# A recurrent attention and a mixture of depths in one kernel: first decays loaded by two queues, two vectors loaded as rows, fewer products of zeros

## The chip, the cores and the metric

The kernel runs on one core of a Trainium2 chip. The metric is the device time of one execution in microseconds (us), as the median of several runs.

## What is computed

The reference chains two blocks. The first is a recurrence with a decay for each channel, over 4 batches, 8 heads, 768 steps and a head width of 48. For each step, with a state of 48x48 for each batch and head:

```python
cur = np.einsum('bhd,bhe->bhde', u[None] * kt, vt)
y[:, :, t] = np.einsum('bhd,bhde->bhe', rt, state + cur)
state = wt[:, :, :, None] * state + np.einsum('bhd,bhe->bhde', kt, vt)
```

Its outputs, the 8 heads side by side, are the rows x (4 batches of 768 rows of 384) of the second block. There each row gets a score `x @ w_gate`. In each batch the 128 rows with the highest scores go through two matrices, `relu(xe @ w1) @ w2` with 1024 in the middle; the result times the sigmoid of the score is added to the row. All other rows are put out as they are. Everything is fp32.

## The kernel before

**Tiling.** The 768 steps of a batch are cut into 6 chunks of 128, so there are 24 chunks, numbered n. For each chunk the kernel loads r, k, v and w as tiles of 128 steps by 8 heads by 48 channels, in buffers with 64 places for each head (`r_bufs`, `k_bufs`, `w_bufs`: 4 each; `v_bufs`: 5). The 16 spare places are filled once (1 for w, 0 for the others) with `nc.any.memset`, which picks an engine (line 130).

**One chunk.** TensorE transposes w (`decays_t`, into `ps_w`), so that the steps lie along the free axis. VectorE runs two scans over the decays (`scans`): `right` at line 255 and `left` at line 266, with two small operations between them. k and r are transposed too (`inputs_t`, into `ps_t`) and multiplied by the scans' results (`scaled`, line 313), which gives `K` and `R`; for the first two chunks `K` is made by a copy on ScalarE (`src`) and a multiplication on GpSimd instead (`scaled_aside`). `scores` multiplies K and R into `ps_s` (line 349), `masked` applies the causal mask on VectorE (`sc`, line 357), and `outputs_t` multiplies by v and by the state into `ps_yt` (lines 382 and 390), which ScalarE copies to `yt`. `ps_s` and `ps_yt` share one buffer of PSUM. `back` transposes K again (copied to `kt` by ScalarE), and `carry_products` and `carry` make the next state. `range_check` runs over w on ScalarE (`junk`, line 302).

**The bonus of u.** The term with u touches a step's own value alone: `own_products` (line 325, r times k) and `own_weights` (line 328, times `u_bc`) on GpSimd, `own_values` (8 sums on ScalarE, line 334), `own_results` on GpSimd. `u_bc` holds u in all 128 partitions; one DMA puts it there, which reads the same 384 values 128 times (`_rows(u, L)`).

**Rows out and scores.** `rows_out` transposes `yt` back, adds the bonus, and stores x. `row_products` multiplies x by `wg_bc` (GpSimd, line 419), the gate's vector in all partitions, which is loaded in the same way. `row_sums` adds up on ScalarE, and `compared` ranks the scores (`ahead`, line 491). `mixture` and `forward` gather the chosen rows and run the two matrices; their products are fed piecewise between those of later chunks.

**Order.** The order is written out by hand. `turn(i)` calls the steps of chunks i-1 to i+2 in the order in which each engine gets them, for i from -2 to 24. All loads and stores are issued by SyncE (SP) in one row, in program order: first the decays of chunk 0 as two halves of the heads, then the list in lines 150 to 161, with `u_bc` after k of chunk 1 and `wg_bc` after w of chunk 3; later loads are issued by `loads(i + 5)` at the end of a turn.

**Products of zeros.** `warm(n)` lets TensorE multiply a tile of zeros (`nothing`, bf16, 128x512) n times into a PSUM tile that nobody reads. It is called with 6 ahead of the first turn, and within the turns -2, -1 and 0:

```python
        if i == 0:
            warm(6)
```

Of the kernel before, what the change touches and what calls it, by code (L numbers as in the profile page):

```python
# [10 lines left out]
FP32 = mybir.dt.float32  # L11
# [7 lines left out]
L = 128  # L19
# [6 lines left out]
def _rows(ap, n):  # L26

    return dataclasses.replace(ap, ap=[[0, n]] + [list(x) for x in ap.ap])
# [10 lines left out]
def kernel(  # L39
# [40 lines left out]
    nc = tc.nc  # L80
    PSUM = bass.MemoryType.PSUM

    B, H, S, D = r.shape
    C = H * D
# [12 lines left out]
    consts = ctx.enter_context(tc.tile_pool(name="consts", bufs=1))  # L97
    setup = ctx.enter_context(tc.tile_pool(name="setup", bufs=1))
# [7 lines left out]
    psM = ctx.enter_context(tc.tile_pool(name="psM", bufs=1, space=PSUM))  # L106
# [14 lines left out]
    r_bufs = [consts.tile([L, H, DP], FP32, name=f"r_buf{i}") for i in range(NBUF)]  # L121
    k_bufs = [consts.tile([L, H, DP], FP32, name=f"k_buf{i}") for i in range(NBUF)]
    w_bufs = [consts.tile([L, H, DP], FP32, name=f"w_buf{i}") for i in range(NBUF)]
    v_bufs = [consts.tile([L, H, DP], FP32, name=f"v_buf{i}") for i in range(VBUF)]
    nothing = setup.tile([L, 512], BF16)
    nc.vector.memset(nothing, 0.0)
    for i in range(VBUF):
# [4 lines left out]
    def load(bufs, x, n):  # L132
        if n < N:
            b, ci = chunks[n]
            nc.sync.dma_start(  # L135
                out=bufs[n % len(bufs)][:, :, 0:D],
                in_=x[b, :, ci * L:(ci + 1) * L, :].rearrange("h t d -> t h d"),
            )

    def loads(n):  # L140
        load(v_bufs, v, n - 2)
        load(k_bufs, k, n - 1)
        load(r_bufs, r, n - 1)
        load(w_bufs, w, n)


    for hs in (slice(H // 2, H), slice(0, H // 2)):
        nc.sync.dma_start(
            out=w_bufs[0][:, hs, 0:D], in_=w[0, hs, 0:L, :].rearrange("h t d -> t h d")
        )  # L150
    for bufs, x, n in (
        (k_bufs, k, 0), (r_bufs, r, 0), (w_bufs, w, 1), (k_bufs, k, 1),
    ):
        load(bufs, x, n)
    u_bc = consts.tile([L, H, D], FP32)
    nc.sync.dma_start(out=u_bc, in_=_rows(u, L))
    for bufs, x, n in ((r_bufs, r, 1), (w_bufs, w, 2), (v_bufs, v, 0)):
        load(bufs, x, n)
    loads(3)
    wg_bc = consts.tile([L, C], FP32)  # L160
    nc.sync.dma_start(out=wg_bc, in_=_rows(moe_w_gate, L))
    w1 = consts.tile([L, NDC, F], FP32)
    w2 = consts.tile([L, NFC, C], FP32)

# [8 lines left out]
    def load_weights(n):  # L173
        while n > 0 and weights:
            to, src = weights.pop(0)
            nc.sync.dma_start(out=to, in_=src)
            n -= 1
# [3 lines left out]
    make_identity(nc, ident)  # L181
    minus = consts.tile([L, 1], BF16)
    nc.vector.memset(minus, -1.0)
    ones_f = consts.tile([L, 1], FP32)
    nc.vector.memset(ones_f, 1.0)
    high = consts.tile([L, 1], FP32)
# [2 lines left out]
    row = setup.tile([L, L], INT32)  # L189
# [6 lines left out]
    for t, sign in ((before_f, 1), (after_f, -1)):  # L196
        nc.gpsimd.memset(t, 1.0)
        nc.gpsimd.affine_select(
            out=t, in_=t, pattern=[[sign, L]], base=-1, channel_multiplier=-sign,
# [32 lines left out]
    def warm(n):  # L232

        ps = psM.tile([L, 512], FP32, tag="m", name="ps_n")
        for _ in range(n):
            nc.tensor.matmul(ps, nothing[:, 0:L], nothing, start=True, stop=True)


    def transposed(pool, tag, src):
# [36 lines left out]
    def check_sums():  # L276

        above = setup.tile([L, 1], FP32)
        nc.vector.tensor_reduce(out=above, in_=guard, axis=AX.X, op=ALU.add)
        below = setup.tile([L, 1], FP32)  # L280
        junk = setup.tile([L, N * HP], FP32)
        nc.vector.tensor_scalar(
            out=junk, in0=alls.rearrange("p n j -> p (n j)"), scalar1=float(LOW ** L),
            scalar2=None, op0=ALU.is_lt, op1=ALU.add, accum_out=below,
        )
        return above, below
# [342 lines left out]
    def step(f, n, *more):  # L629
        if 0 <= n < N:  # L630
            f(work.setdefault(n, dict(n=n)), *more)

    def mix(n=1, place=None):


        while n > 0 and mixing:
            if place is not None and mixing[0][1] not in (None, place):
                return
            try:
                mixing[0][1] = next(mixing[0][0])  # L640
                n -= 1
            except StopIteration:
                mixing.pop(0)
# [16 lines left out]
    def fed_in_turn(n, few):  # L660

        kept = (feed or picked) and (feed or picked)[0][0] == B - 2
        fed(few if kept else n, on=False)
# [6 lines left out]
    def turn(i):  # L670
        soon = i >= N - 1
        step(first_left, i + 1)
        if i < 1:
            step(scaled_aside, i + 1, "K", "right")
        step(own_products, i + 1)
        step(scores, i)
        step(own_values, i)
        step(carry, i - 1, work.get(i))
        if i > 0:
            step(scaled, i + 1, "K", "right")  # L680
        step(own_weights, i + 1)
        if soon:
            step(masked, i)
        if i == N - 1:
            sums.extend(check_sums())
        if i < N:
            step(compared, i - 2)
        if not soon:
            step(masked, i)
        step(back, i)  # L690
        if i == 0:
            warm(6)
        mix(place="half")
        step(rows_out, i - 1, soon)
        step(row_scores_soon if soon else row_products, i - 1)
        step(own_results, i)
        fed_in_turn(PIECES // 2, 2 if i >= N - 1 else 1)
        step(inputs_t, i + 1, "R", r_bufs)
        if i == -1:
            warm(2)  # L700
        step(scaled, i + 1, "R", "left")
        step(decays_t, i + 2)
        mix(place="mid")
        if i == -2:
            warm(2)
        step(range_check, i + 2)
        step(outputs_t, i)
        step(carry_products, i)
        fed_in_turn(PIECES - PIECES // 2, 1 if i == N - 1 else 0)
        if i == N - 1:  # L710
            step(compared, i - 1)
        step(inputs_t, i + 2, "K", k_bufs)
        if i == -2:
            warm(1)
        if not soon:
            step(row_sums, i - 1)
        step(scans, i + 2)
        if 0 <= i - 2 < N - 1 and chunks[i - 2][1] == NCH - 1:
            mixing.append([mixture(chunks[i - 2][0]), "end"])
        mix(place="end")  # L720
        if i > -2:
            loads(i + 5)
        if i in WEIGHT_TURNS:
            load_weights(1)

    with tc.manual_schedule():
        warm(6)
        for i in range(-2, N + 1):
            turn(i)

        ended.append(True)
        mix(1000)
        mixing.append([mixture(B - 1), "half"])
        step(compared, N - 1)
        fed(1)
        mix()
        wide = checked(sums)
        fed(1)
        mix()
        fed(NFC - 2)  # L740
        mix(2)
        fed(2)
        mix(1000)
        fed(1000)
        outside = nc.values_load(wide, min_val=0, max_val=1)
# [72 lines left out]
```

## Time and profile before

| | |
|---|---|
| time, median of 3 runs | 205.34 us (205.33 to 205.54) |
| the profiled execution's own time | 205.87 us |
| its span in the profile | 204.2 us |
| busy in the span: TensorE (PE) | 191.8 us (94%) |
| VectorE (DVE) | 160.8 us (79%) |
| GpSimd (POOL) | 135.7 us (66%) |
| ScalarE (ACT) | 124.6 us (61%) |
| loads and stores on SP's queue | 27.14 MB, 73.6% of 16 DMA engines' span |
| chain that ended last, by engine | PE 77%, SP's queue 7%, DMA 6%, DVE 4% |

In the profile's lines the first number is the start and the second the duration, both in us from the span's start; then come the engine, the line of the kernel, the operation and the tiles, written tile first. "xN" is the number of instructions merged into a line. In square brackets stands how long the engine was idle ahead of the line, and what ended that. "SPq" is SyncE issuing a DMA. In a table of windows each engine has its busy time and, in brackets, its number of instructions in that stretch; the last three columns are the granted clock, the DMA share and GB/s.

### The profile page before, as it was taken

Reading aid. Unit: us, or ns where it says so; the run is one execution under the profiler, and the core shown is the slowest. Engines: PE = TensorE matmul, PEld = TensorE weight load, DVE = VectorE, ACT = ScalarE, POOL = GpSimd, SP = SyncE. Lnnn points to the kernel's source line nnn. Section 1 sums busy time; section 2 is a strip of 40 time slices with the busy share of each in tenths; the row PEclk is TensorE's granted clock in tenths of the full one; section 3 lists DMA queues with packets and bytes.
Section 4 is the critical chain, followed back from the end, with each engine's and each line's share of the span. In section 5 each row is a group of like instructions: output and inputs, shape, how many; then the busy total and the mean of one; then the engine's idle time right before and its main releaser. Section 6 shows DMA issues by size and latency. Waiting matters only on the chain.

```text
span 204.2 us, 6418 instructions
## 1 busy us (share of the span) xinstructions
PE 191.8 (94%) x2292; PEld 156.2 (76%) x2293; DVE 160.8 (79%) x352; ACT 124.6 (61%) x644; POOL 135.7 (66%) x167
## 2 busy tenths in 40 slices
PE   7999999999899899999999999999999999999980
PEld 3577888877687688888877888898887888876940
DVE  5989899999999968988969788988879784961010
ACT  7287877768954776868454866878355866510300
POOL 6586898886867995777538898678528898111301
PEclk9999999999999999999999999999999999999997
DMA  6999999798989999999992994978672221111101
GB/s 111 186 163 173 176 187 204 173 223 151 257 161 251 171 216 218 174 206 240 200 199 57 189 171 108 154 146 158 126 121 65 55 79 42 39 42 42 39 8 43
DMA packets 105671, 29.20 MB, mean 143 GB/s; under 512 B 100512, under 2 KB 104864, under 8 KB 105632
## 3 DMA queue, kind: packets, MB, share of 16 engines
q1 hardware_dynamic: 105120, 27.14, 73.6%
q0 software_dynamic: 512, 1.57, 2.6%
q8 instruction: 20, 0.33, 0.8%
q14 instruction: 19, 0.16, 0.3%
HBM read 23.20 MB, written 5.51 MB: 141 GB/s over the span
## 4 chain that ended last, share of the span: by engine, by line
PE 77%; SPq 7%; DMA 6%; DVE 4%; ACT 2%; issue 2%; POOL 0%; POOLq 0%; DVEq 0%; ACTq 0%
PE ps_t L242 12%; PE ps_h L595 11%; PE ps_f L607 11%; PE ps_s L349 11%; PE ps_yt L382 10%; DMA k_buf<-in_k_dram 6%; SPq L135 5%; PE ps_yt L390 5%; PE ps_y L242 5%; PE ps_w L242 4%; PE ps_kv L444 4%; PE ps_e L485 3%; PE ps_r L511 1%; PE ps_x L559 1%; DVE left L266 1%
## 5 line engine op out<-in xcount | busy, mean ns | idle before, releaser
L334 ACT ACTIVATE rk<-rk 128x48 f32<-128x48 f32 x192 | 43.7, 231 | 0.0
L414 POOL TENSOR_TENSOR x<-x,vo 128x384 f32<-128x384 f32 x22 | 22.1, 1007 | 21.6 <-ACT x L412 21.3
L334 ACT ACTIVATION_READ_ACCUMULATOR rk<-rk 128x1 f32 x192 | 36.3, 189 | 0.0
L266 DVE TENSOR_TENSOR_SCAN left<-ps_w,from_left 128x511 f32<-128x511 f32 x24 | 30.7, 1280 | 0.9
L395 ACT COPY yt<-ps_yt 128x512 f32<-128x512 f32 x24 | 14.1, 586 | 27.6 <-PE ps_yt L390 24.8
L255 DVE TENSOR_TENSOR_SCAN right_buf<-ps_w,from_right 128x511 f32<-128x511 f32 x24 | 29.1, 1211 | 1.8 <-PE ps_w L242 1.7
L357 DVE TENSOR_TENSOR sc<-ps_s,before_f 128x1024 f32<-128x1024 f32 x24 | 29.3, 1219 | 0.8 <-PE ps_s L349 0.8
L349 PE MATMUL ps_s<-R,K 48*128 48x128 f32 x384 | 27.9, 285 | 0.3 <-ACT yt L395 0.2
L382 PE MATMUL ps_yt<-sc,v_buf 128*64 128x128 f32 x384 | 26.3, 278 | 1.4 <-PE ps_w L242 1.2
L349 PEld LDWEIGHTS ps_s<-R,K 48*128 48x128 f32 x384 | 23.3, 187 | 3.9 <-issue 2.7
L325 POOL TENSOR_TENSOR rk<-r_buf,k_buf 128x384 f32<-128x384 f32 x24 | 24.2, 1007 | 2.6 <-DMA r_buf<-in_r_dram 2.6
L595 PE MATMUL ps_h<-xeT,w 128*128 128x128 f32 x192 | 25.5, 280 | 0.2 <-ACT hid L600 0.2
L382 PEld LDWEIGHTS ps_yt<-sc,v_buf 128*64 128x64 f32 x384 | 20.6, 136 | 5.6 <-issue 3.0
L328 POOL TENSOR_TENSOR rk<-rk,u_bc 128x384 f32<-128x384 f32 x24 | 24.2, 1008 | 0.7
L595 PEld LDWEIGHTS ps_h<-xeT,w 128*128 128x128 f32 x192 | 22.9, 192 | 1.6 <-ACT xeT L561 0.5
L607 PE MATMUL ps_f<-w,hid 128*128 128x384 f32 x64 | 23.8, 499 | 0.0
L419 POOL TENSOR_TENSOR scr<-x,wg_bc 128x384 f32<-128x384 f32 x22 | 22.0, 1000 | 1.7
L340 POOL TENSOR_TENSOR vo<-v_buf,own 128x384 f32<-128x384 f32 x24 | 19.9, 831 | 1.3 <-ACT rk L334 1.3
L313 DVE TENSOR_TENSOR R<-ps_t,left 128x512 f32<-128x512 f32 x24 | 16.5, 687 | 4.6 <-ACT own L573 1.6
L313 DVE TENSOR_TENSOR K<-ps_t,right_buf 128x512 f32<-128x512 f32 x22 | 15.0, 684 | 5.1 <-PE ps_t L242 5.1
L242 PE MATMUL ps_t<-ident,k_buf 128*128 128x128 f32 x96 | 15.4, 284 | 1.3 <-DMA k_buf<-in_k_dram 1.3
L242 PE MATMUL ps_w<-ident,w_buf 128*128 128x128 f32 x96 | 15.3, 284 | 1.0 <-ACT every L496 0.7
(103 smaller groups left out, 350.1 us busy)
## 6 DMA issues: line engine op xcount, KB each, us to landing
k_buf<-in_k_dram SPq DMA_DIRECT2D x24, 192.0 KB, 5.1
r_buf<-in_r_dram SPq DMA_DIRECT2D x24, 192.0 KB, 5.2
v_buf<-in_v_dram SPq DMA_DIRECT2D x24, 192.0 KB, 4.6
out_dram<-x SPq DMA_DIRECT2D x24, 192.0 KB, 3.5
w_buf<-in_w_dram SPq DMA_DIRECT2D x23, 192.0 KB, 4.8
w<-in_moe_w_dram SPq DMA_DIRECT2D x3, 512.0 KB, 5.6
w<-in_moe_w_dram SPq DMA_DIRECT2D x4, 384.0 KB, 5.0
w_buf<-in_w_dram SPq DMA_DIRECT2D x2, 96.0 KB, 2.5
```

The source lines that it names most:

```text
L242: nc.tensor.transpose(ps[:, j, :], src(j), ident)
L255: nc.vector.tensor_tensor_scan(out=flat[:, W - 2::-1], data0=wt[:, W - 1:0:-1], data1=from_right.rearrange("p j t -> p (j t)")[:, W - 2::- ...
L266: nc.vector.tensor_tensor_scan(out=left.rearrange("p j t -> p (j t)")[:, 1:W], data0=wt[:, 0:W - 1], data1=start.rearrange("p j t -> p (j ...
L313: nc.vector.tensor_mul(out, t.pop(name + "t"), t.pop(by))
L325: nc.gpsimd.tensor_mul(rk, r_bufs[n % NBUF][:, :, 0:D], k_bufs[n % NBUF][:, :, 0:D])
L328: nc.gpsimd.tensor_mul(t["rk"], t["rk"], u_bc)
L334: nc.scalar.activation(out=rk[:, h, :], in_=rk[:, h, :], func=AF.Copy, accum_out=o[:, h:h + 1])
L349: nc.tensor.matmul(ps[:, q, j, :], t["K"][rows, j, :], t["R"][rows, j, :], start=True, stop=True,)
L357: nc.vector.tensor_mul(t["sc"].rearrange("p q j t -> p (q j) t"), ps.rearrange("p q j t -> p (q j) t"), _heads(before_f, 2 * HP),)
L382: nc.tensor.matmul(ps[half(c), j % 2, j // 2, :], vt[:, 2 * j + q, :], t["sc"][:, q, j, :], start=(j < 2), stop=(old is None), skip_group_ ...
L595: nc.tensor.matmul(ps[:, q, :], w1[:, dc, (f0 + q) * L:(f0 + q + 1) * L], xeT[:, dc, :], start=(dc == 0), stop=(dc == NDC - 1),)
L607: nc.tensor.matmul(ps, hid[:, fc, :], w2[:, fc, :], start=(fc == 0), stop=(fc == NFC - 1))
```

## The change

The two halves of the first decays are issued by two queues: heads 4 to 7 by SP, heads 0 to 3 by ScalarE's queue, ahead of everything else. ScalarE's queue then loads u and the gate's vector as one row each (1x384). SP's list loses both broadcast loads. A new function `spread` multiplies a row of 128 ones (one partition) by such a row, which puts it in all 128 partitions of a PSUM tile, and ScalarE copies that to `u_bc` or `wg_bc`. In turn -1 u is spread after `range_check`, and `own_weights` of chunk 0 follows it there; in turn 0 the gate is spread after the zero products. `warm` is called with 2 instead of 6 in turn 0, with 1 instead of 2 in the middle of turn -2, and no longer at the end of turn -2 (1) and in turn -1 (2). The 6 ahead of the first turn stay.

```diff
+    for queue, hs in ((nc.sync, slice(H // 2, H)), (nc.scalar, slice(0, H // 2))):
+        queue.dma_start(
+            out=w_bufs[0][:, hs, 0:D], in_=w[0, hs, 0:L, :].rearrange("h t d -> t h d")
+        )
+
+    u_row = setup.tile([1, C], FP32)
+    nc.scalar.dma_start(out=u_row, in_=_rows(u.rearrange("h d -> (h d)"), 1))
+    wg_row = setup.tile([1, C], FP32)
+    nc.scalar.dma_start(out=wg_row, in_=_rows(moe_w_gate, 1))
+    u_bc = consts.tile([L, H, D], FP32)
+    wg_bc = consts.tile([L, C], FP32)
     nothing = setup.tile([L, 512], BF16)
...
-    for hs in (slice(H // 2, H), slice(0, H // 2)):
-        nc.sync.dma_start(
-            out=w_bufs[0][:, hs, 0:D], in_=w[0, hs, 0:L, :].rearrange("h t d -> t h d")
-        )
     for bufs, x, n in (
-        (k_bufs, k, 0), (r_bufs, r, 0), (w_bufs, w, 1), (k_bufs, k, 1),
+        (k_bufs, k, 0), (r_bufs, r, 0), (w_bufs, w, 1), (k_bufs, k, 1), (r_bufs, r, 1),
+        (w_bufs, w, 2), (v_bufs, v, 0),
     ):
         load(bufs, x, n)
-    u_bc = consts.tile([L, H, D], FP32)
-    nc.sync.dma_start(out=u_bc, in_=_rows(u, L))
-    for bufs, x, n in ((r_bufs, r, 1), (w_bufs, w, 2), (v_bufs, v, 0)):
-        load(bufs, x, n)
     loads(3)
-    wg_bc = consts.tile([L, C], FP32)
-    nc.sync.dma_start(out=wg_bc, in_=_rows(moe_w_gate, L))
...
+    one_row = setup.tile([1, L], FP32)
+    nc.vector.memset(one_row, 1.0)
...
+    def spread(to, row):
+
+        ps = psM.tile([L, C], FP32, tag="m", name="ps_b")
+        nc.tensor.matmul(ps, one_row, row, start=True, stop=True)
+        nc.scalar.copy(out=to, in_=ps)
...
-        step(own_weights, i + 1)
+        if i >= 0:
+            step(own_weights, i + 1)
...
         if i == 0:
-            warm(6)
+            warm(2)
+            spread(wg_bc, wg_row)
...
         step(inputs_t, i + 1, "R", r_bufs)
-        if i == -1:
-            warm(2)
...
         if i == -2:
-            warm(2)
+            warm(1)
         step(range_check, i + 2)
+        if i == -1:
+            spread(u_bc.rearrange("p h d -> p (h d)"), u_row)
+            step(own_weights, i + 1)
...
         step(inputs_t, i + 2, "K", k_bufs)
-        if i == -2:
-            warm(1)
```

## The prediction

> **What bounds the kernel now.** I read the windows first, because the edits all lie in the first 20 us: which engine is full there, and afterwards?
>
> ```profile
> core 0: us, PE busy (x) PEld busy (x) DVE busy (x) ACT busy (x) POOL busy (x), PEclk, DMA share, GB/s
> 4.90:24.00 19.10, 17.70 (x194) 13.47 (x194) 17.30 (x26) 12.32 (x68) 13.07 (x14) 1.00 1.28 175
> 24.00:74.00 50.00, 46.69 (x657) 38.68 (x655) 48.66 (x99) 36.21 (x192) 41.27 (x48) 1.00 1.02 200
> 74.00:172.00 98.00, 98.00 (x1233) 82.66 (x1231) 82.11 (x172) 65.21 (x347) 71.54 (x80) 1.00 0.77 143
> ```
>
> From 24 to 74 us DVE is full (48.66 of 50), from 74 to 172 PE is (98.00 of 98). So a lead of DVE's work at 24 us should be carried to the end, unless something else catches it. The chain of waits tells another story of the start:
>
> ```profile
> 13.93 1.14 SPq L161
> 15.59 6.20 DMA k_buf<-in_k_dram
> 21.93 0.63 PE ps_t L242 x4
> 22.55 1.09 PE ps_s L349 x16
> ```
>
> It runs over SP's DMA issues to k of chunk 3, which lands at 21.79, and then over PE. But PE waited only 0.19 us for that load. Which engine really sets the pace I take from DVE's timeline, of which these are the only four rows with a wait before them:
>
> ```profile
> 4.90 1.22 DVE L255 TENSOR_TENSOR_SCAN right_buf<-ps_w,from_right 128x511 f32<-128x511 f32 x1 [1.42 <-PE ps_w L242]
> 13.25 0.69 DVE L313 TENSOR_TENSOR R<-ps_t,left 128x512 f32<-128x512 f32 x1 [0.37 <-PE ps_t L242]
> 19.09 0.69 DVE L313 TENSOR_TENSOR R<-ps_t,left 128x512 f32<-128x512 f32 x1 [0.28 <-PE ps_t L242]
> 23.94 0.35 DVE L491 SCALAR_TENSOR_TENSOR ahead<-ps_e,score,after_f 128x128 bf16<-128x128 f32 x1 [0.45 <-PE ps_e L485]
> ```
>
> From 4.90 on DVE runs nearly without a break. All that an edit of the start can win is in these waits, all for PE: 1.42, 0.37, 0.28 and 0.45 us. PE's timeline says why each is there:
>
> ```profile
> 1.27 2.74 PE L236 MATMUL ps_n<-nothing 128*128 128x512 bf16 x6 [1.27 <-DVE high L187]
> 3.80 1.06 PE L242 MATMUL ps_w<-ident,w_buf 128*128 128x128 f32 x4
> 6.98 0.70 PE L242 MATMUL ps_t<-ident,r_buf 128*128 128x128 f32 x4
> 11.26 1.46 PE L236 MATMUL ps_n<-nothing 128*128 128x512 bf16 x5
> 12.56 0.60 PE L242 MATMUL ps_t<-ident,r_buf 128*128 128x128 f32 x4
> 15.82 0.63 PE L242 MATMUL ps_t<-ident,k_buf 128*128 128x128 f32 x4 [0.75 <-DMA k_buf<-in_k_dram]
> 16.38 1.16 PE L349 MATMUL ps_s<-R,K 48*128 48x128 f32 x16
> 18.40 0.60 PE L242 MATMUL ps_t<-ident,r_buf 128*128 128x128 f32 x4
> ```
>
> The 0.37 is the six zero products of turn 0, behind which r of chunk 1 waits until 12.56 although it landed at 10.9. The 0.28 is k of chunk 2: PE waits 0.75 us for it, and scores, back-transposes, outputs and r of chunk 2 all follow late. The 0.45 is the same lateness one chunk on.
>
> **First decays by two queues.** The halves land at 3.1 (issue 0.82 + 2.3) and 4.0 (1.32 + 2.7). I expect both at 3.1 to 3.5. It gains nothing at the first scan: PE starts these transposes at 3.80, when the six zero products of the prologue are through, and those stay. Price 0; the cover is those products, and if the half on ACT's queue landed later than the 4.0 of now, DVE would start that much later. ACT's three issues stand ahead of its table load. No ACT issue is in the trace; by SP's rows they cost 0.4 to 1.14 us each, so 1.3 to 3.4 us. ACT now idles 1.53 us before 6.57. At 1.3 us nothing is late. At 3.4 us the copy `src` moves from 6.80 to about 7.9 and `K` of chunk 0 on POOL from 8.74 to 9.8, where the scores end at about 11.0, still before DVE takes them at 11.68. Price 0 at both ends. In the changed program's order DVE clears 12 buffers instead of 8 ahead of its first scan; they start 0.14 us apart now, so DVE is ready at about 4.1 instead of 3.5, hidden by the same products until 4.90.
>
> The skill's page "DMA: Bandwidth & Descriptors", section "Issuing engines are not separate DMA queues", speaks against this edit: two issuers share the same 16 engines, and only issue time is saved. By the rule the sum would be the same.
>
> **u and gate as rows.** SP loses two issues. The 192 KB of u land 0.7 us after k of chunk 1 (5.00 + 4.7 = 9.7 against 4.05 + 4.9 = 9.0), a load of the same size in 192-byte pieces takes 1.2 us (r of chunk 1, 6.19 + 4.7 = 10.9). So everything behind u comes 0.7 us earlier, behind gate again 0.7, and the half of w that left SP's queue gives 0 to 0.9 (the distance of the two halves). k of chunk 2 comes at 14.1 to 15.0 instead of 15.7, k of chunk 3 near 20. At either end PE's 0.75 us wait goes; next late is `yt` of chunk 0, whose buffer the scores need: ACT copies it at 14.66 to 15.25. ACT gets the copy of gate just before it, about 0.48 us (`xeT`, 128x384 from PSUM, 0.479), which fits in the 0.62 us that ACT idles there. So scores of chunk 1 start at about 15.2, not 16.38, and DVE, which can take them at about 17.2, doesn't wait.
>
> The two products are 128x384 fp32 with one row of weights. The nearest row is `ps_f`, 128x384, 16 in 5.18 us, 0.32 us each; doubled while the clock is half, 0.65. I take 0.32. That of u stands between the transposes of w (chunk 1) and k (chunk 1), where PE idles 0.41 us waiting for k. Its copy on ACT falls into ACT's 1.80 us idle before 10.48, and POOL's multiplication with u, now later in the order but with only own products ahead of it, runs at 9.8 as before if the copy is through by then (about 9.4). Price 0. Behind a late copy POOL's next `K` at 11.24 would queue, which has until about 15.
>
> **Fewer zero products.** Turn 0 loses four. At 0.216 us each (7.52 to 7.74 in the instruction starts) that is 0.86, and the gate product takes 0.32: r of chunk 1 could start 0.5 us earlier, and another 0.4 because the scores before it no longer wait for k. DVE is done with the masked scores at 12.88, so R starts there: the whole 0.37 goes. The three taken in turns -2 and -1 are off DVE's path: R of chunk 0 at 7.98 waits for the left scan that ends at 7.85.
>
> **Sum.** 0.37 + 0.28 + 0.45 = 1.10, of which I keep 1.0, since the last is three engines long (ACT's row sums, POOL's gate products, PE). The first 1.42 stays. The profiled execution took 205.87 (span 204.20), so 204.87; its own time is 0.53 above the median of 205.34, from which I forecast **204.35**.
>
> **What is not in the trace: the clock.** The first four transposes took 1.06 us, those of r at 6.98 took 0.70, later ones 0.60 to 0.63; by the starts they are 0.213 us apart until 6.98 and 0.109 from 7.3. So PE runs at half rate until about 7.2 us, although it has been busy since 1.27, and fewer products might leave it there longer. (The granted clock in the windows reads 1.00 all along, so I go by the starts.) From 3.80 to 7.2 PE now idles about 0.2 us; after the change I expect about 0.4, waiting for r of chunk 0.
>
> The page "TensorE: Matmul & The Clock Gate", sections "What's actually happening" and "Part 4: PE-mode transpose", speaks against the change: the gate opens after a busy window of about 3.4 us, and transposes do not count. Here the run of six zero products (2.5 us up to 3.80) did not open it and a stretch made mostly of transposes did, which speaks against the second part. By the page, an estimate is that the gate opens one window later, near 10.6.
>
> **Rivals.** *A somewhat later clock* (rises near the scores of chunk 0): only the transposes of w (chunk 1) take 0.43 longer, right scan 0.3 late, gain 0.7: 204.65. *The clock stays half through turn 0* (the other side): transposes of w from 8.05 take 0.86, u 0.65, k 0.86, scores 2.0, back 0.86, two zero products 0.85, gate 0.35 to 0.65, r 0.43: R of chunk 1 at 15.2 instead of 13.25, 2.0 late; 0.73 of the later waits go, net +1.3, **206.6**. It decides once R of chunk 1 starts later than 13.25 + 0.73 = 14.0. For it: three zero products fewer before 7.2, and up to 1 us of idle PE before w of chunk 1. Against: PE stays nearly as busy. *Lead lost*: loads or instruction fetch hold the pace between 24 and 74 us (DMA share 1.02 there): 205.3. Against: behind 23.94 DVE has no wait over 0.3 there, and k of chunk 4 lands at 26.5, 1.3 us before PE takes it. *More*: overlaps at the four waits give 1.4: 203.9.
>
> **Numbers.** Forecast (204.1 to 204.6) 0.52; later clock or part of the waits 0.15; lost 0.14; slow clock, +0.4 to +2, 0.15; more 0.04. About 0.2%, 0.41 us, is what a measurement can tell. Faster 0.67, same 0.15, slower 0.18. The range 203.9 to 206.0 leaves out the top of the slow case and the bottom of the last, under 0.2.
>
> **What would show it.** Right: first scan still at 4.9, clock at full rate by 7.5, R of chunk 1 near 12.8 with no wait, k of chunk 2 landed by 15.0, no DVE wait at R of chunk 2, `ahead` near 22.8, and DVE's 24-to-74 stretch 1 us earlier. Wrong: transposes 0.213 apart after 8 us; ACT's table load after 5 us; a first scan after 5; `yt` of chunk 0 later than 15; or all this kept and a new wait behind 24 us.

## The result, and the profile after

The changed kernel took 205.24 us (median, 205.19 to 205.29), the kernel before 205.43 on the same chip: 0.19 us less, ratio 0.9990, 95% interval 0.9973 to 1.0008, which by itself does not exclude that nothing changed. A second series on another chip (after_again below) gives 205.32 against 205.62, ratio 0.9984 (0.9974 to 0.9993). So the change gains 0.2 to 0.3 us where 1.0 was forecast; the range of 203.9 to 206.0 holds the time. In 5 of the 14 executions of the second series the kernel took 208.4 to 210.0 us, and one that was traced shows TensorE's clock falling back at 10.06 us; the ratios, here and below, leave such executions out, while the medians hold them.

The windows of the kernel after, same columns as before:

```profile
core 0: us, PE busy (x) PEld busy (x) DVE busy (x) ACT busy (x) POOL busy (x), PEclk, DMA share, GB/s
4.90:24.00 19.10, 17.12 (x193) 13.29 (x195) 17.40 (x28) 13.86 (x76) 14.11 (x15) 1.00 1.38 163
24.00:74.00 50.00, 46.81 (x659) 38.94 (x658) 48.12 (x97) 36.57 (x197) 40.59 (x46) 1.00 1.14 213
74.00:172.00 98.00, 97.90 (x1235) 82.46 (x1235) 82.49 (x172) 64.86 (x341) 71.78 (x81) 1.00 0.72 137
```

Behind 24 us hardly anything has changed. DVE's timeline shows what did change ahead of it; here are its first scan, R of chunks 1 and 2, and the first ranks:

```profile
4.64 1.22 DVE L266 TENSOR_TENSOR_SCAN right_buf<-ps_w,from_right 128x511 f32<-128x511 f32 x1 [0.47 <-PE ps_w L253]
13.63 0.69 DVE L324 TENSOR_TENSOR R<-ps_t,left 128x512 f32<-128x512 f32 x1 [1.01 <-PE ps_t L253]
19.07 0.68 DVE L324 TENSOR_TENSOR R<-ps_t,left 128x512 f32<-128x512 f32 x1
23.46 0.35 DVE L502 SCALAR_TENSOR_TENSOR ahead<-ps_e,score,after_f 128x128 bf16<-128x128 f32 x1
```

Two of the four waits are gone (0.28 at R of chunk 2, 0.45 at the ranks). One has grown: R of chunk 1 waits 1.01 us instead of 0.37. And the first scan comes 0.26 earlier, which was not forecast. TensorE's timeline has the reason for the 1.01:

```profile
8.38 0.91 PE L246 MATMUL ps_b<-u_row,one_row 1*128 1x384 f32 x2
9.22 0.66 PE L253 MATMUL ps_t<-ident,k_buf 128*128 128x128 f32 x4
11.39 0.38 PE L241 MATMUL ps_n<-nothing 128*128 128x512 bf16 x1
12.04 0.91 PE L246 MATMUL ps_b<-wg_row,one_row 1*128 1x384 f32 x2 [0.27 <-PE ps_t L253]
12.88 0.66 PE L253 MATMUL ps_t<-ident,r_buf 128*128 128x128 f32 x4
15.38 0.66 PE L253 MATMUL ps_t<-ident,k_buf 128*128 128x128 f32 x4
```

The chain of waits, which ran over SP's issues up to 15 us before, now holds both products with ones:

```profile
8.45 0.84 PE ps_b L246 x2
...
12.04 0.91 PE ps_b L246 x2
```

Each product with ones stands as two records ("x2"), two passes of TensorE for one fp32 product. By the starts a pass takes 0.43 us, so a product holds TensorE 0.84 us (8.38 to 9.22, and 12.04 to 12.88). From the end of the back-transposes to r of chunk 1 it is 1.49 us now (11.39 to 12.88), and it was 1.30 with six zero products (11.26 to 12.56).

The two profiles' spans differ by 0.70 us (204.17 against 203.47). Masked scores of chunk 0 start 0.26 earlier (11.68, 11.42), of chunk 1 0.35 later (17.59, 17.94), of chunk 2 0.47 earlier; these are the lines of chunk 2, before and after:

```profile
24.21 1.22 DVE L357 TENSOR_TENSOR sc<-ps_s,before_f 128x1024 f32<-128x1024 f32 x1
23.74 1.22 DVE L368 TENSOR_TENSOR sc<-ps_s,before_f 128x1024 f32<-128x1024 f32 x1
```

This 0.47 stands unchanged up to chunk 9. At chunk 10 it is 0.74: the execution of before lost 0.28 more near 70 us, at no edit of the change, and no other profile has this. If the 0.26 of the first scan is taken off the 0.47, 0.21 is left for the edits, which agrees with the medians.

### The profile page after: what moved, and what is told of

Read it like the earlier page. It is cut to its first block, busy times and chain, and to the rows that moved or that the text cites. A ratio compares the mean times of both kernels' runs of the same rounds, so it can differ in the third digit from the quotient of the medians.

```text
span 203.5 us, 6413 instructions
## 1 busy us (share of the span) xinstructions
PE 190.5 (94%) x2288; PEld 154.9 (76%) x2289; DVE 161.4 (79%) x357; ACT 124.2 (61%) x642; POOL 135.5 (67%) x167
## 4 chain that ended last, share of the span: by engine, by line
PE 85%; DVE 4%; DMA 3%; ACT 2%; POOL 2%; issue 2%; SPq 1%; POOLq 0%; DVEq 0%; ACTq 0%
PE ps_t L253 14%; PE ps_s L360 12%; PE ps_h L606 11%; PE ps_f L618 11%; PE ps_yt L393 11%; PE ps_w L253 5%; PE ps_yt L401 5%; PE ps_y L253 5%; PE ps_kv L455 5%; PE ps_e L496 3%; DMA w_buf<-in_w_dram 3%; PE ps_r L522 1%; PE ps_b L246 1%; ACT rk L345 1%; PE ps_x L570 1%
## 5 line engine op out<-in xcount | busy, mean ns | idle before, releaser
L313 ACT ACTIVATE junk<-w_buf,high 128x384 f32<-128x384 f32 x24 | 15.1, 630 | 1.0 <-DMA w_buf<-in_w_dram 0.7
```

## The experiments

### One part alone

few_zeros takes the fewer zero products into the kernel before, and nothing else:

```diff
-            warm(6)
+            warm(2)
...
-        if i == -1:
-            warm(2)
...
-            warm(2)
+            warm(1)
...
-        if i == -2:
-            warm(1)
```

> The kernel before with the fewer zero products alone (2, 1, 0 and 0 instead of 6, 2, 2 and 1 in the turns). Theory A (TensorE's chain, with two links: in turn 0 the products ahead of r of chunk 1, then the landing of k of chunk 2): R of chunk 1 starts 0.4 us earlier on VectorE (12.8 to 12.9 if the first scan stays at 4.9), but k of chunk 2 still lands at 15.7, so scores of chunk 1 stay at 16.4, R of chunk 2 waits about 0.7 instead of 0.28, and nothing is left of the gain behind it: 205.4, within 0.2 of before. Rival B (each wait counts by itself, as in the prediction's sum): the 0.37 is kept, 205.0. Rival C (clock): with fewer zero products full rate comes later or not before 10 us: 205.7 or more.

205.66 against 205.61, ratio 1.0003 (0.9994 to 1.0012). DVE's rows with a wait behind the first scan:

```profile
17.54 1.22 DVE L357 TENSOR_TENSOR sc<-ps_s,before_f 128x1024 f32<-128x1024 f32 x1 [0.34 <-PE ps_s L349]
19.05 0.69 DVE L313 TENSOR_TENSOR R<-ps_t,left 128x512 f32<-128x512 f32 x1 [0.28 <-PE ps_t L242]
24.13 0.35 DVE L491 SCALAR_TENSOR_TENSOR ahead<-ps_e,score,after_f 128x128 bf16<-128x128 f32 x1 [0.58 <-PE ps_e L485]
```

R of chunk 1 no longer waits, so the 0.37 was really won there. It is given back at once: TensorE gets k of chunk 2 at 15.77 (15.82 before), now after waiting 0.85 us, and the masked scores of chunk 1 start only 0.05 earlier. The waits don't add up; they stand in a row, and the load sets the second one. B is out, and so is C: full rate came at 6.78 us.

no_u_load also leaves u's load away, so the bonus term is missing from its result:

```diff
-    nc.sync.dma_start(out=u_bc, in_=_rows(u, L))
+    nc.gpsimd.memset(u_bc, 0.0)
```

> few_zeros with u's load left out: u's tile is filled with zeros on GpSimd, so the bonus term is left out of the result. Theory A (the second link is k of chunk 2 behind u's load): k of chunk 2 lands at 14.9 to 15.1 instead of 15.7, no wait at the scores of chunk 1 nor at R of chunk 2, masked scores of chunk 2 0.8 to 1.0 earlier than in few_zeros, 204.6 to 204.8. Rival: the loads don't matter, 205.4 to 205.6 as few_zeros.

k of chunk 2 lands at 15.04 and is taken at 15.18 instead of 15.77, the masked scores of chunks 1 and 2 start 0.57 and 0.59 earlier than in few_zeros. That is the direction of theory A, at two thirds of its size: the ranks still wait 0.58, because k of chunk 3 (taken at 21.52 after 0.52 of waiting) still stands behind the gate's load. The time, 205.29 against 205.62, ratio 0.9996 (0.9977 to 1.0016), doesn't settle it.

two_queues is the kernel before with the two halves of the first decays on two queues:

```diff
+    for queue, hs in ((nc.sync, slice(H // 2, H)), (nc.scalar, slice(0, H // 2))):
+        queue.dma_start(
...
-    for hs in (slice(H // 2, H), slice(0, H // 2)):
-        nc.sync.dma_start(
...
```

> The kernel before with the first decays alone issued by two queues. Theory A: the first transposes wait for the six zero products at 3.8, and loads behind come 0.1 to 0.25 us earlier: 205.4, within 0.2 of before. Rival D (the 0.26 us that the first scan came earlier in the changed kernel is the work of the second queue): first scan at 4.6 instead of 4.9, 205.15.

205.44 against 205.61, ratio 0.9997 (0.9985 to 1.0008): nothing that can be told. The first scan started at 5.11, not 4.6, so D is out: the 0.26 us of the changed kernel's profile is not the second queue's. It rather delays that scan. Among the profiles whose clock rose later than 5 us, the first scan starts at 4.90 to 4.91 in the four kernels that load both halves by SP, and at 4.98 to 5.11 in the six that use two queues. In two_queues the first transposes start at 3.98 instead of 3.80; SP's half landed at 3.85, where it had landed at 3.07 before.

rows_only has the rows and their products, but all zero products and both halves on SP:

```diff
-    for queue, hs in ((nc.sync, slice(H // 2, H)), (nc.scalar, slice(0, H // 2))):
+    for queue, hs in ((nc.sync, slice(H // 2, H)), (nc.sync, slice(0, H // 2))):
...
-            warm(2)
+            warm(6)
             spread(wg_bc, wg_row)
...
```

> The kernel after with all zero products of before put back and both halves of the first decays on SP: rows and their products with ones alone. Theory A: the gate product stands behind six zero products, R of chunk 1 starts about 0.85 us later than in the kernel after (near 14.4), k of chunk 2 lands by 15.1 and the waits at R of chunk 2 and at the ranks are gone, so masked scores of chunk 2 are about 0.4 later than before: 205.8. Rival L (the loads alone set the pace, the products don't count): 205.2, as the kernel after.

206.06 against 205.61, ratio 1.0025 (1.0016 to 1.0034), 0.45 us slower. R of chunk 1 waits 1.87 us:

```profile
14.62 0.69 DVE L324 TENSOR_TENSOR R<-ps_t,left 128x512 f32<-128x512 f32 x1 [1.87 <-PE ps_t L253]
```

It is the only wait left behind the first scan; the loads do come in time. The masked scores of chunk 2 start 0.51 us later than before. So the products cost what the earlier loads win, and more. L is out. The edits need each other: the fewer zero products without the rows give 0, the rows without the fewer zero products lose 0.45, both together gain 0.2 to 0.3.

### The gate's product out of the way

gate_late moves it to where TensorE waits for k of chunk 2:

```diff
         if i == 0:
             warm(2)
-            spread(wg_bc, wg_row)
...
         step(carry_products, i)
+        if i == 0:
+            spread(wg_bc, wg_row)
```

> The kernel after with the gate's product moved behind the carry products of turn 0, where TensorE waits for k of chunk 2. Theory A (the gate's product, 0.84 us and 0.22 of waiting ahead of it, on the path to r of chunk 1, took the gain): R of chunk 1 starts at 12.5 to 12.7 without a wait, masked scores of chunk 2 0.6 to 0.9 us earlier than in the kernel after, and that lead is kept to the end: 204.4 to 204.6. Rival E (the lead is lost behind 24 us, on loads or instruction fetches): R of chunk 1 early, but 205.1 to 205.3.

204.86 against 205.61, ratio 0.9957 (0.9943 to 0.9972). The median is that of six executions, of which four took 204.74 to 204.88 and two 207.85 and 208.19; the ratio, of the four alone, is 0.88 us. TensorE's timeline:

```profile
12.06 0.60 PE L253 MATMUL ps_t<-ident,r_buf 128*128 128x128 f32 x4
14.50 0.91 PE L246 MATMUL ps_b<-wg_row,one_row 1*128 1x384 f32 x2
15.34 0.66 PE L253 MATMUL ps_t<-ident,k_buf 128*128 128x128 f32 x4
```

r of chunk 1 starts at 12.06 instead of 12.88, DVE has no wait at R of chunk 1, and k of chunk 2 still comes at 15.34, as in the kernel after. The lead over before is 0.77 us at the masked scores of chunk 2 and no smaller at those of chunk 23. So one line moved by half a turn gives most of the gain that was forecast for the whole change, and it is kept to the end: E is out.

rows_early moves both products into the load waits of turns -2 and -1, ahead of k and r of chunk 0:

> The kernel after with both products moved up: u's takes the place of the one zero product in turn -2, the gate's stands at the start of turn -1, ahead of r of chunk 0; TensorE waits for loads there. Theory A: R of chunk 1 starts at 12.5 to 12.8 without a wait, scores of chunk 0 no longer behind u's product, time 204.5 to 204.8, as gate_late or 0.1 better. Rival C2: while the clock is at half rate the products take 1.7 us each, r of chunk 0 and left scan's product come late, 205.2 or more.

206.68 against 205.62, ratio 1.0050 (1.0038 to 1.0062): slower by 1.0, the worst of all. Rival C2 holds, more strongly than it was stated:

```profile
4.87 1.64 PE L246 MATMUL ps_b<-u_row,one_row 1*128 1x384 f32 x2
7.49 1.64 PE L246 MATMUL ps_b<-wg_row,one_row 1*128 1x384 f32 x2
10.28 0.69 DVE L324 TENSOR_TENSOR R<-ps_t,left 128x512 f32<-128x512 f32 x1 [2.35 <-PE ps_t L253]
```

Each product takes 1.6 us at half rate, and the clock rose only at 13.7 us here. DVE waits 2.35 us for R of chunk 0.

full_rows puts an idle product with all 128 rows in the place of gate_late's two zero products, to price the one-row product against it:

```diff
-            warm(2)
+            ps = psM.tile([L, C], FP32, tag="m", name="ps_d")
+            nc.tensor.matmul(
+                ps, ident, from_right.rearrange("p j t -> p (j t)")[:, 0:C], start=True, stop=True
+            )
```

> gate_late with the two zero products of turn 0 replaced by one idle fp32 product of 128 x 128 by 128 x 384, of the same moving size as the gate's but with all 128 rows. It prices a product: theory A1 (two passes of 0.32, as the pair of records in the expert's second product): 0.65 us in two records 0.32 apart, against 0.84 of the one-row products (0.42 apart). Rival A2 (any fp32 product of 384 columns that stands alone costs 0.84): 0.42 apart here too. Time as gate_late within 0.2, R of chunk 1 0.2 to 0.4 later on TensorE, still without a wait on VectorE.

The profiled execution ran at half rate there:

```profile
13.55 1.49 PE L705 MATMUL ps_d<-from_right,ident 128*128 128x384 f32 x2
```

Compared at half rate, its two passes start 0.64 apart (13.551, 14.192), those of the one-row product in rows_early 0.80 (4.874, 5.675). At full rate the one-row passes are 0.43 apart and those of `ps_f` 0.32. So A1 holds against A2: a product that stands alone also takes two passes of the shorter kind, and a one-row pass is longer by a quarter to a third. Why, no run shows. At full rate the idle product was not traced, nor were the waits that were expected with it. In five of nine executions the kernel took 208.2 us or more, so its median is 208.19; the other four took 204.88 to 205.03, and their ratio is 0.9967 (0.9953 to 0.9981), near gate_late's.

### The clock

after_again is the kernel after, unchanged:

> The kernel after, unchanged, in more runs. Theory A: waits at R of chunk 2 and at the ranks gone (0.28 + 0.45), R of chunk 1 0.4 to 0.6 later by the gate's product, net gain 0.2 us, so 205.2 to 205.4 where before is 205.4 to 205.6. Rival C (the clock's rise at 3.9 us in the profile, 3.2 us earlier than in the profile of before, is due to the change): again a rise near 4 us and a first scan at 4.6 to 4.7. If the rise only falls on a beat of 3.41 us that runs freely, it lies elsewhere this time.

The median agrees with theory A, and rival C is out: the clock rose at 6.65 us this time, the first scan started at 5.10. But the profiled execution took 209.91 us, and its windows, cut where the trace's clock records change, show why:

```profile
6.65:10.06 3.41, 2.54 (x14) 1.55 (x14) 3.22 (x4) 1.80 (x5) 2.22 (x2) 1.00 1.53 163
10.06:13.47 3.41, 3.41 (x23) 2.78 (x22) 2.83 (x4) 2.83 (x20) 3.16 (x3) 0.50 1.53 163
13.47:16.89 3.42, 3.36 (x10) 1.64 (x9) 0.02 (x1) 1.45 (x4) 2.37 (x4) 0.50 1.53 163
16.89:20.30 3.41, 3.41 (x36) 3.07 (x34) 3.13 (x5) 0.68 (x4) 1.46 (x2) 0.50 1.53 166
```

The clock is up for one stretch of 3.41 us and then at half rate for three. TensorE is busy throughout the half-rate stretches, DVE starves in the second (0.02 of 3.42 us). The scores take 2.08 us instead of 1.16, the gate's product 1.64, and R of chunk 1 starts at 16.96:

```profile
10.14 2.08 PE L360 MATMUL ps_s<-R,K 48*128 48x128 f32 x16
16.96 0.69 DVE L324 TENSOR_TENSOR R<-ps_t,left 128x512 f32<-128x512 f32 x1 [3.47 <-ACT junk L313]
```

The profile names ScalarE's `junk` for that wait; TensorE's transposes of r, from 15.75 to 16.86, end just before R and fit it better.

Two kernels test whether the removed zero products are what kept it up. Both put back the four that the change takes out of turns -2 and -1, so that five stand there again, after_zeros into the kernel after, keep_clock into gate_late:

```diff
+        if i == -1:
+            warm(2)
         step(scaled, i + 1, "R", "left")
...
-            warm(1)
+            warm(2)
...
+        if i == -2:
+            warm(1)
...
```

> The kernel after with the five zero products of turns -2 and -1 put back; turn 0 keeps two and the gate's product. Theory A with the clock: median as the kernel after, 205.1 to 205.4, and no execution at 208 or more. Rival G: executions at 208 or more stay, in about one of four.

> gate_late with the zero products of turns -2 and -1 put back (2, 1 and 2, as before the change); turn 0 keeps its two. Theory A with the clock: these five stand where TensorE waits for loads, off VectorE's path, so the time of undisturbed executions stays at 204.7 to 204.9; and with them the clock, once up, keeps full rate, so no execution is at 208 or more. Rival F (they delay w of chunk 1 or u's product): 205.0 to 205.3. Rival G (the clock's fall in some executions has nothing to do with TensorE's idle time there): executions at 208 and more as in the kernel after.

after_zeros: 205.19 against 205.50, ratio 0.9983 (0.9974 to 0.9992). keep_clock: **204.70** against 205.50, ratio 0.9961 (0.9948 to 0.9975). None of their 16 executions took more than 205.32, nor did F's delay show: keep_clock is the fastest of all versions. Its DVE rows with a wait, and the masked scores of chunk 2:

```profile
4.65 1.22 DVE L266 TENSOR_TENSOR_SCAN right_buf<-ps_w,from_right 128x511 f32<-128x511 f32 x1 [0.48 <-PE ps_w L253]
18.27 0.69 DVE L324 TENSOR_TENSOR R<-ps_t,left 128x512 f32<-128x512 f32 x1 [0.28 <-PE ps_t L253]
22.88 0.35 DVE L502 SCALAR_TENSOR_TENSOR ahead<-ps_e,score,after_f 128x128 bf16<-128x128 f32 x1 [0.22 <-PE ps_e L496]
23.16 1.22 DVE L368 TENSOR_TENSOR sc<-ps_s,before_f 128x1024 f32<-128x1024 f32 x1
```

after_zeros and keep_clock differ in the gate's product alone, and their medians put its price in its old place at 0.49 us. The profile of keep_clock can be set beside that of the kernel after, since both have their first scan at 4.64 to 4.65: masked scores of chunk 2 start at 23.16 instead of 23.74, which is 0.58 us, though these two kernels also differ by the four zero products.

G is unlikely, but not excluded. Executions of 207.8 us or more came in 5 of 14 of after_again, 2 of 6 of gate_late and 5 of 9 of full_rows, in none of the 4 of the first series of the kernel after and in none of the 16 with the zero products put back; but these 16 ran on another chip. The fewer zero products alone do not bring it about: few_zeros has none in 11. Nor does it seem to take a product with ones: in no_u_load, which has none, two of twelve executions took 206.80 us with a granted clock of 0.978 and 0.980, where the other ten have 0.992 to 0.996. Neither was traced.

## Why the prediction was wrong

**The step that failed first: the price of a product with ones.** In the prediction, "16 in 5.18 us, 0.32 us each" took 16 records for 16 products. They are 8 products of two passes, 0.65 each. The page of the profile before could have told it: `ps_f` has 64 records for 4 batches of 8 products. A one-row product took 0.84. Ahead of the gate's one comes another 0.22, in which TensorE seems to wait for its own last zero product to leave the PSUM buffer that both use. That product has no record; by the spacing it starts at 11.61 and ends 0.38 later, 0.05 ahead of 12.04. In rows_only and after_again the gate's product also starts 0.06 after the last zero product ends, while in gate_late, behind products into another buffer, it starts before they end (14.50 against 14.57). So the gate's part of turn 0 costs 1.06 instead of 0.32, against 0.86 for the four zero products: the edit that was to win 0.5 us there loses 0.2. Moving this one product away brought 0.5 us (keep_clock against after_zeros), so this step is shown by a run.

**The same error hid u's product.** It was to fit in TensorE's 0.41 us wait for k of chunk 1. With 0.84 it makes k 0.1 later (9.22 against 9.12) although k landed at 8.89; the "another 0.4 because the scores before it no longer wait for k" did not come. This is read from the trace; no run moves u's product alone at full rate. In all, r of chunk 1 would by the prediction's terms have started at about 11.7 and came at 12.88.

**The sum of the waits.** 0.37 + 0.28 + 0.45 took three waits for independent. few_zeros shows them in a row: what is won at the first is lost at the second as long as u's load stands ahead of k of chunk 2. The rule would have been: a lead counts as far as the next late thing lets it. For the whole change it did no harm, since both links were to be mended.

**What held.** The loads: k of chunk 2 landed at 14.9 (predicted 14.1 to 15.0), all behind u came 0.7 to 0.8 earlier, and k of chunk 3, behind the gate's load too, 1.2 (20.59 against 21.79). ACT's three issues took 0.48, 0.67 and 0.23 us, near the lower end of 1.3, and hid nothing. The waits at R of chunk 2 and at the ranks vanished. DVE's lead at chunk 2 was kept to the end. With the product out of the way the gain was 0.8 of the 1.0 forecast (keep_clock).

**What else was off.** The two halves of the first decays did not land at 3.1 to 3.5: in after_again they landed at 3.84 (SP) and 4.17 (ScalarE's queue), against 3.07 and 4.02 before. So the second queue made the first scan 0.1 to 0.2 us later at the same clock, where its price was put at 0. The scan came 0.26 earlier in the profile of the kernel after because the clock happened to rise early in that execution, which is luck. The changed program has four zero products fewer in turns -2 and -1, not three, of which two stood ahead of 7.2 us. And the time is where the rival "lead lost" had it (205.3), but not by its mechanism: the small lead that there was is kept behind 24 us.

**The clock.** The rival had it stay at half rate until turn 0. What happens instead in some executions: it rises as early as ever and falls back one stretch later. That TensorE idles more between its short jobs, with the loads in hand and fewer zero products, fits the counts above, but which executions fall stays open. The price was larger than estimated (R of chunk 1 at 16.96 in after_again, 15.2 in the rival), and the ratios leave it out.

## What to carry to other kernels

Before a product is priced from a row of the profile, count the records against the products of the code: an fp32 product is two records here. An operation that replaces another is to be put where its engine waits, not where the old one stood; the same 0.84 us cost about 0.5 us more in one place than in another. And zero products that seem idle may hold the clock: take them from the path, but leave them in the waits.

## What the runs showed of the hardware

**The clock changes on a beat of its own.** By the trace's clock records the full-rate stretches last whole multiples of 3.413 us: 194.56 in before (57), 197.97 in after (58), 3.41 and 184.32 in after_again (1 and 54). The rise came at 7.18 us in the profile of before, 3.93 in that of after, and between 4.2 and 7.2 in the others except rows_early (13.7). So the 0.26 us of the first scan is a matter of where the beat fell: the other profile with an early rise, keep_clock at 4.23, has it at 4.65 too. The Trainium skill, page "TensorE: Matmul & The Clock Gate", section "What's actually happening", states a freely running window of 3413 ns; the traces agree.

**Transposes count as work.** The same page, section "Part 4: PE-mode transpose", says that the full clock does not engage for transposes, which don't count as busy in the same way. In few_zeros the clock rose at 6.78, after a beat in which, by the starts of the products, transposes filled half and zero products a quarter; a beat filled to 0.73 by zero products alone raised nothing in the profile of before. The measurement decides: these transposes count.

**How busy is busy enough is only bounded.** A beat's filling is here the time from the start of each product to that of the next, without the pauses; a pass ahead of a pause counts with the spacing that its kind has in a row. The beat of before from 0.35 to 3.76, 0.73 filled with zero products, raised nothing; every beat at whose end the clock rose was filled to 0.75 or more. Two beats at full rate were followed by a fall (after_again about 0.63, full_rows 0.51), but the kernel after kept its clock at 0.44 and few_zeros at 0.52. Both beats that fell hold u's one-row product; without it they are at 0.38 and 0.33. In rows_early two beats of over 0.9, with 1.6 us of a one-row product in each, raised nothing. That one-row products count for little would sort these, but after_again's beat from 10.06, busy 0.88 with scores of 48 rows, raised nothing either, and the two executions of no_u_load with the lower clock have no one-row product. How rows enter stays open; no run was made for it.
